# Nine edits to the order of work in a fused Fourier-mixing and SoLU kernel

## The chip, the cores and the metric

The kernel runs on one core of a Trainium2 chip. The metric is the device time of one execution in microseconds (us). The core has five engines that run side by side, each with its own instruction queue in program order: TensorE (PE, matrix products; its weight loads are listed as PEld), VectorE (DVE), ScalarE (ACT), GpSimd (POOL) and SyncE (SP, which here only issues DMAs). ACT and POOL issue DMAs too. [...]

## The reference

```python
X = np.fft.rfft(x, axis=1)                    # x: 8 x 3136 x 256
y = np.fft.irfft(X * (filt_r + 1j * filt_i), n=3136, axis=1)
x = y.reshape(25088, 256)
h = x @ w_in                                  # 256 -> 1024
e = np.exp(h - np.max(h, axis=-1, keepdims=True))
solu = h * (e / (np.sum(e, axis=-1, keepdims=True) + 1e-09))
mu = np.mean(solu, axis=-1, keepdims=True)
var = np.mean((solu - mu) ** 2, axis=-1, keepdims=True)
out = ((solu - mu) / np.sqrt(var + 1e-06) * g_ln) @ w_out   # 1024 -> 256
```

## The kernel before

**Two halves that overlap.** A prologue (up to about 150 us) transforms sequence 0 and prepares weights. Then one loop, `step(k)`, k from 0 to 204, carries 196 blocks of 128 tokens through the SoLU part, while the Fourier work of sequences 1 to 7 is dealt out into the same steps by the table `PLAN`. Two steps make a pair j (k = 2j is even, k = 2j + 1 is odd), since both products are done in Strassen's manner: seven products instead of eight for two blocks. Four blocks make a group g.

**The SoLU pipeline.** Steps 2j and 2j + 1 compute `product(j, 1..7)` into PSUM. The even step runs products 1, 2, 6, 7 and the odd one 5, 3, 4. Products 1, 6, 5, 3 pile up in one bank (`ms[j, 0]`); after each but the last, `keep` (ACT, L738) copies the running sum out, so the next product into that bank waits for the copy. `finish` (DVE, L749 and L752) adds the other banks. Two steps later `exponential` (ACT, L760) and `normalize` (DVE, L771 to L776) make the SoLU; three steps later `turn` (DVE, L792) transposes 32 x 32 blocks and `square` (ACT, L784) sums the variance. For a pair p = j - 3 the even step `regroup`s (eight DMAs on SP, L804) the turned blocks into `solu_t`; `project_sums` (POOL, L707) makes Strassen's sums from it. `project(p, m)` (PE, L849) multiplies by `w_out`: products 1, 2, 6, 7 of pair p = j - 4 in the odd step, and 5, 3, 4 of p = j - 5 in the even one. `keep_out` (ACT, L861) and `finish_out` (DVE, L865) scale the result by the row's 1/sigma, and `store_out` (two DMAs on SP, L873) writes it.

**The row factors.** 1/sigma of group g takes a detour through DRAM, since it has to be turned from rows to the regrouped order. `deviations` (two small POOL operations L811, L813 and one SP DMA, L815, `rows<-rs`) runs in even step 4g + 6. `regroup_deviations` (four SP DMAs of 0.5 KB, L821, `rs_t<-rows`) runs in odd step 4g + 7. The first reader is `keep_out(p, 0, (0, 0))` of p = 2g, right after `project(p, 1)` in odd step 4g + 9.

**The Fourier part.** At the end of a step stand `late`, `pcs`, `pas`, `pbs`, `pys`, in this order: pc is the inverse product of a spectrum unit (its two PSUM banks are copied out by ACT, L344), pa the first stage (copied by ACT, L269), pb the forward spectrum product, py the last stage (copied by ACT, L382, and joined by DVE, L390). pc and pb use the same two banks `ps_b`, one buffer each; pa and py share the two buffers of `ps_t`. `spectrum_loads` issues from ACT's queue the two loads of a spectrum unit (512 KB of `t2`, L286, and 256 KB of tables, L688), in the step before that unit's pb.

**What sets the order.** `tc.manual_schedule()`: every engine executes its instructions in the order in which `step` writes them. [...]

## Time and profile before

| | us |
|---|---|
| median of 3 runs | 1702.94 (1692.59 to 1709.13) |
| the profiled execution | 1712.57 |
| its span | 1710.8 |
| PE busy, share of the span | 1571.6, 92% |
| DVE busy | 1315.0, 77% |
| POOL busy | 1132.6, 66% |
| ACT busy | 906.7, 53% |

The difference of span and execution, 1.8 us, lies around the program. PE's busy time is partly modelled, so 92% says that PE rarely sits idle, not that it runs at its peak. In the chain of waits, which follows what ended last back to the start, the PE lines of the two token products, L849 and L728, hold 23% and 22% of the span, and DMAs 21%. The granted PE clock is full for all of the stretch from 550 to 1650 us. From about 1300 us on the Fourier work is over and only the SoLU part runs: there one sees a group of four steps undisturbed, 26.9 us long (the `turn` of 1516.3 and that of 1543.2 stand at the same place of the pattern).

### The profile page before, as it was taken

The page shows a single profiled execution, that of the slowest core. Times are in us where ns is not written, and L with a number is a line of the kernel's source. Part 1 is how long each engine was busy: PE and PEld are TensorE (multiplying, and loading weights), DVE is VectorE, ACT ScalarE, POOL GpSimd, SP SyncE. Part 2 cuts the span into 40 slices and gives each one's busy share as a digit, 9 for nine tenths or more (in the row PEclk, how much of TensorE's full clock was granted, in tenths as well). Part 3 has the DMA queues.
Part 4 walks back from the last instruction along what each step waited for, and adds up shares of the span by engine and source line. Part 5 has one row for each costly group of instructions (what it writes and reads, how often), then busy time and mean ns, then how long its engine had stood idle before and what let it go on. Part 6 is the DMA issues. An engine that isn't in the chain of part 4 may idle for free.

```text
span 1710.8 us, 36980 instructions
## 1 busy us (share of the span) xinstructions
PE 1571.6 (92%) x12710; PEld 1074.3 (63%) x12710; DVE 1315.0 (77%) x2642; ACT 906.7 (53%) x1772; POOL 1132.6 (66%) x1316
## 2 busy tenths in 40 slices
PE   5897889999889999999999999999999999999986
PEld 1353456666556676666666676666666677666666
DVE  1676877886678889887898788987888777777772
ACT  2134554565445655565556555565555565555552
POOL 4443686777566776787578766687666767666564
PEclk8999999999999999999999999999999999999998
DMA  9887877876788768865887678866775455343343
GB/s 259 250 269 228 239 208 201 220 209 167 170 223 200 195 188 233 225 182 150 201 239 193 171 175 220 220 180 166 199 223 133 123 127 121 101 100 97 94 106 93
DMA packets 377805, 312.13 MB, mean 182 GB/s; under 512 B 63322, under 2 KB 343395, under 8 KB 377619
## 3 DMA queue, kind: packets, MB, share of 16 engines
q1 hardware_dynamic: 306260, 169.81, 39.4%
q0 software_dynamic: 34464, 101.68, 20.8%
q10 hardware_dynamic: 36896, 38.28, 7.7%
q8 instruction: 103, 1.69, 0.4%
q14 instruction: 82, 0.67, 0.1%
HBM read 124.86 MB, written 81.50 MB: 121 GB/s over the span
## 4 chain that ended last, share of the span: by engine, by line
PE 54%; DMA 21%; DVE 11%; issue 6%; SPq 2%; ACT 2%; POOL 2%; ACTq 0%; DVEq 0%; POOLq 0%
PE o L849 23%; PE m L728 22%; DMA solu_t<-turn 6%; DMA x<-in_x_dram 3%; PE pb L296 2%; PE py L377 2%; DVE h L776 2%; DMA rs_t<-rows 2%; PE pc L296 2%; DMA t<-d 2%; DMA d<-x 2%; PE pa L264 2%; DMA rows<-rs 2%; DVE turn L792 1%; SPq L804 1%
## 5 line engine op out<-in xcount | busy, mean ns | idle before, releaser
L728 PE MATMUL m<-w_in_sb,s 128*128 128x512 f32 x784 | 397.1, 606 | 36.2 <-ACT h L738 28.9
L849 PEld LDWEIGHTS o<-w_out_sb,solu_t 128*128 128x128 f32 x3136 | 385.1, 194 | 54.4 <-issue 43.1
L849 PE MATMUL o<-w_out_sb,solu_t 128*128 128x128 f32 x3136 | 404.0, 278 | 8.3 <-DVE ot L865 8.3
L849 PEld LDWEIGHTS o<-w_out_sb,u 128*128 128x128 f32 x2352 | 307.6, 192 | 146.6 <-issue 129.9
L849 PE MATMUL o<-w_out_sb,u 128*128 128x128 f32 x2352 | 310.7, 275 | 10.0 <-ACT ot L861 10.0
L728 PE MATMUL m<-w_in_sb,y 128*128 128x512 f32 x588 | 310.3, 611 | 2.2 <-DVE nmax L752 2.2
L776 DVE SCALAR_TENSOR_TENSOR h<-e,rsum,h 128x1024 f32<-128x1024 f32 x196 | 306.6, 1564 | 6.9
L707 POOL TENSOR_TENSOR u<-solu_t 128x512 f32<-128x512 f32 x98 | 135.4, 1382 | 265.4 <-DMA solu_t<-turn 218.7
L861 ACT ACTIVATE ot<-o,rs_t 128x128 f32<-128x128 f32 x392 | 144.7, 369 | 265.2 <-PE o L849 240.5
L738 ACT COPY h<-m 128x512 f32<-128x512 f32 x294 | 171.1, 582 | 198.4 <-PE m L728 195.4
L784 ACT ACTIVATE h<-h,nmu 128x1024 f32<-128x1024 f32 x196 | 224.4, 1145 | 90.1 <-DVE turn L792 44.5
L792 DVE STREAM_TRANSPOSE turn<-h 128x1024 f32<-128x1024 f32 x196 | 242.5, 1237 | 2.1 <-DVE ot L865 0.3
L760 ACT ACTIVATE e<-h,nmax 128x1024 f32<-128x1024 f32 x196 | 224.9, 1148 | 22.4 <-DVE h L776 22.3
L728 PEld LDWEIGHTS m<-w_in_sb,s 128*128 128x128 f32 x784 | 130.5, 192 | 149.5 <-issue 96.8
L865 DVE SCALAR_TENSOR_TENSOR ot<-o,rs_t,ot 128x128 f32<-128x128 f32 x294 | 101.0, 344 | 148.8 <-ACT ot L861 121.9
L752 DVE CUSTOM_DVE_ANT_0 h<-m,h 128x512 f32<-128x512 f32 x196 | 134.2, 685 | 91.4 <-ACT h L738 88.0
L707 POOL TENSOR_TENSOR u<-solu_t,u 128x512 f32<-128x512 f32 x98 | 143.8, 1467 | 70.2 <-PE o L849 65.0
L707 POOL TENSOR_TENSOR solu_t<-solu_t,solu_t 128x512 f32<-128x512 f32 x98 | 142.5, 1454 | 7.7
L707 POOL TENSOR_TENSOR u<-u,solu_t 128x512 f32<-128x512 f32 x98 | 144.1, 1470 | 0.5
L728 PEld LDWEIGHTS m<-w_in_sb,y 128*128 128x128 f32 x588 | 96.7, 191 | 74.8 <-issue 49.1
L707 POOL TENSOR_TENSOR s<-y 128x128 f32<-128x128 f32 x196 | 100.4, 512 | 0.5
L318 DVE TENSOR_TENSOR pr<-pb,f 128x512 f32<-128x512 f32 (+1 forms) x53 | 34.3, 648 | 83.7 <-PE pb L296 60.3
(112 smaller groups left out, 2045.2 us busy)
## 6 DMA issues: line engine op xcount, KB each, us to landing
solu_t<-turn SPq DMA_DIRECT2D x784, 128.0 KB
out_dram<-ot SPq DMA_DIRECT2D x196, 128.0 KB
t<-d POOLq DMA_DIRECT2D x112, 200.0 KB, 6.0
d<-x POOLq DMA_DIRECT2D x100, 200.0 KB, 4.7
f<-f_dram POOLq DMA_DIRECT2D x39, 512.0 KB, 6.9
d<-g POOLq DMA_DIRECT2D x39, 512.0 KB, 4.9
t<-d ACTq DMA_DIRECT2D x36, 512.0 KB
x<-in_x_dram SPq DMA_DIRECT2D x112, 98.0 KB
```

What stands on the lines that cost most here:

```text
L296: nc.tensor.matmul(out=out[:, v, :], lhsT=lhsT(v), rhs=rhs[:, v, :], start=True, stop=True)
L707: nc.gpsimd.tensor_tensor(out=out, in0=in0, in1=in1, op=op)
L728: nc.tensor.matmul(out=ms[j, bank], lhsT=lhsT, rhs=w_in_sb[:, w, :], start=m in (1, 2, 7), stop=True, skip_group_check=True)
L738: nc.scalar.copy(out=h_half(k, i), in_=ms[j, 0])
L752: nc.vector.tensor_tensor_reduce(out=h_half(k, i), in0=ms[j, bank], in1=h_half(*kept), scale=1.0, scalar=sofar, op0=ALU.add, op1=ALU.min, ...
L760: nc.scalar.activation(out=e, in_=hs[k], func=AFT.Exp, bias=nmaxs.pop(k)[:, 1:2], scale=-1.0, accum_out=esum)
L776: nc.vector.scalar_tensor_tensor(out=solu, in0=e, scalar=rsum, in1=solu, op0=ALU.mult, op1=ALU.mult, accum_out=nmu)
L784: nc.scalar.activation(out=solu, in_=solu, func=AFT.Square, bias=nmu, scale=-float(DFF), accum_out=variances[g][:, i:i + 1])
L792: nc.vector.transpose(out=turns[g][:, :, i, :], in_=solus[k].rearrange("p (f j) -> p f j", j=32))
L849: nc.tensor.matmul(out=pos[p, bank], lhsT=lhs[:, f, :], rhs=w[:, f, :], start=f == 0 and m in (1, 2, 7), stop=True, skip_group_check=True)
L861: nc.scalar.activation(out=out_half(p, *to)[0], in_=pos[p, 0], func=AFT.Copy, scale=rs)
L865: nc.vector.scalar_tensor_tensor(out=ot, in0=pos[p, bank], scalar=rs, in1=out_half(p, *kept)[0], op0=ALU.mult, op1=ALU.add)
```

## The change

It moves work without changing what is computed:

1. `weight_sums(w_out_sb)`, four DVE subtractions at the end of step 5, becomes four POOL subtractions, one at the end of each of steps 4 to 7.
2. For sequence 1 in steps before 9, the closing add of a spectrum multiplication goes from DVE to POOL, and its second half from the end of step t to the start of step t + 1 (`tops`).
3. Even step: `exponential(k - 2)` goes behind `product(j, 1)` and `keep(j, k, 0)`.
4. Even step: `spectrum_loads` goes from behind `keep_out(p, 1, (0, 1))` to behind `project(p, 4)`, ahead of the regroups.
5. Even step: `regroup(j - 3, 0)` goes down to stand just ahead of `regroup(j - 3, 1)`.
6. `deviations(g)` goes from even step 4g + 6 to the start of odd step 4g + 7.
7. `regroup_deviations(g)` goes from odd step 4g + 7 to the very end of even step 4g + 8, behind `store_out`.
8. End of a step without pa: py goes ahead of pb.
9. In a step with pa but neither pb nor pc, py takes the two `ps_b` banks instead of `ps_t`.

```diff
+    def weight_sum(engine, w, n):
+        to, a, b = ((3, 6, 0), (5, 2, 6), (4, 2, 3), (6, 1, 4))[n]
+        engine.tensor_tensor(out=w[:, to], in0=w[:, a], in1=w[:, b], op=ALU.subtract)
...
-            weight_sums(w_out_sb)
+            weight_sum(nc.gpsimd, w_out_sb, step - 3)
...
-            parts = [lambda sp=sp, i=i, part=part: sp.multiply(i, part) for part in range(2)]
+            add = (nc.gpsimd if t + 1 < LAG else nc.vector).tensor_tensor
+            parts = [lambda sp=sp, i=i, part=part, add=add: sp.multiply(i, part, add) for part in range(2)]
...
-                (first_parts[t] if t + 1 < LAG else second_parts[t + 1]).append(parts[1])
+                (tops if t + 1 < LAG else second_parts)[t + 1].append(parts[1])
...
-            (pys[at] if e > 1 else late[t] if second_one else early[t]).append(lambda e=e, ch=ch: back_halves(
-                e, ch, [psum(f"py_{e}_{ch}_{g}") for g in range(2)]))
+            (pys[at] if e > 1 else late[t] if second_one else early[t]).append(
+                lambda e=e, ch=ch, at=at: back_halves(e, ch, psum_pair(f"py_{e}_{ch}", False)
+                                                      if pas[at] and not pbs[at] + pcs[at] else
+                                                      [psum(f"py_{e}_{ch}_{g}") for g in range(2)]))
...
-        for job in top[k] + stores[k] + differences[k] + products[k]:
+        for job in tops[k] + top[k] + stores[k] + differences[k] + products[k]:
             job()
         if odd and j + 1 < pairs:
             pair_sums(j + 1)
+        if odd and 0 <= j - 3 < pairs:
+            deviations(j - 3)
         if not odd:
-            if 2 <= k < blocks + 2:
-                exponential(k - 2)
             if hid:
                 product(j, 1)
                 keep(j, k, 0)
+            if 2 <= k < blocks + 2:
+                exponential(k - 2)
             if proj:
                 project(p, 5)
                 keep_out(p, 1, (0, 1))
-            for job in spectrum_loads[k]:
-                job()
...
-            if 0 <= j - 3 < pairs:
-                regroup(j - 3, 0)
...
                 project(p, 4)
+            for job in spectrum_loads[k]:
+                job()
             if 0 <= j - 3 < pairs:
+                regroup(j - 3, 0)
                 regroup(j - 3, 1)
-                deviations(j - 3)
...
                 store_out(p)
+            if 0 <= j - 4 < pairs and j % 2 == 0:
+                regroup_deviations((j - 4) // 2)
         else:
...
                 project_sums(j - 3, 0)
-                if (j - 3) % 2 == 0:
-                    regroup_deviations((j - 3) // 2)
...
-        for job in late[k] + pcs[k] + pas[k] + pbs[k] + pys[k] + loads[k]:
+        for job in late[k] + pcs[k] + (pas[k] + pbs[k] + pys[k] if pas[k] else pys[k] + pbs[k]) + loads[k]:
             job()
-        if k in (0, 1, 3, 5):
-            prepare_w_out((k + 1) // 2)
+        if k in (0, 1, 3, 4, 5, 6, 7):
+            prepare_w_out(k - (k > 2))
```

## The prediction

> **What bounds the kernel.** I read the page first: its engine line, the groups, then the chain of waits.

> ```profile
> span 1710.8 us, 36980 instructions
> PE 1571.6 (92%) x12710; PEld 1074.3 (63%) x12710; DVE 1315.0 (77%) x2642; ACT 906.7 (53%) x1772; POOL 1132.6 (66%) x1316
> ...
> L728 PE MATMUL m<-w_in_sb,s 128*128 128x512 f32 x784 | 397.1, 606 | 36.2 <-ACT h L738 28.9
> ```

> PE sets the time: 139 us of idle in 1711, some 46 of them before 155 us. The third line is the largest single idle of the loop: 28.9 us of waiting for `keep`. So every edit is priced by what it does to PE's queue. I then went through PE's list of waits, and next to the timelines of SP, PE and ACT over one undisturbed group, because edits 6 and 7 move DMAs on SP that ACT, and behind it PE, wait for. First SP (start, us, what, count):

> ```profile
> 1517.66 6.00 SPq L804 DMA_DIRECT2D solu_t<-turn  x8
> 1523.75 0.56 SPq L815 DMA_DIRECT2D rows<-rs  x1
> 1524.41 1.31 SPq L873 DMA_DIRECT2D out_dram<-ot  x2
> 1525.82 1.87 SPq L821 DMA_DIRECT2D rs_t<-rows  x4
> 1527.80 9.43 SPq L804 DMA_DIRECT2D solu_t<-turn  x8
> 1537.33 1.30 SPq L873 DMA_DIRECT2D out_dram<-ot  x2
> ```

> This is group 42: step 4g+6 ends with the first stores, 4g+7 is the four `rs_t` loads, 4g+8 is the second eight regroups and the second stores. The reader, on PE and ACT:

> ```profile
> 1533.57 1.06 PE L849 MATMUL o<-w_out_sb,solu_t 128*128 128x128 f32 x8
> 1534.46 1.88 PE L728 MATMUL m<-w_in_sb,s 128*128 128x512 f32 x4
> 1536.18 1.95 PE L849 MATMUL o<-w_out_sb,solu_t 128*128 128x128 f32 x16
> ...
> 1539.68 1.05 PE L849 MATMUL o<-w_out_sb,u 128*128 128x128 f32 x8
> ```
> ```profile
> 1536.38 0.58 ACT L738 COPY h<-m 128x512 f32<-128x512 f32 x1 [2.24 <-PE m L728]
> 1537.27 0.37 ACT L861 ACTIVATE ot<-o,rs_t 128x128 f32<-128x128 f32 x1 [0.31 <-PE o L849]
> 1537.54 1.14 ACT L760 ACTIVATE e<-h,nmax 128x1024 f32<-128x1024 f32 x1
> ```

> PE's lines are project 4 of step 4g+8; products 7 and 5; project 1 and 2 of step 4g+9; and, at 1539.68, project 6, which adds into the bank that `keep_out` must first have read. The reader of `rs_t` is the L861 at 1537.27. The loads ended issuing at 1527.7: even 3.3 us to land leaves 6 us to spare.

> [...] one `rs_t` load is a 0.47 us slice, while the chain of waits shows 3.3 us and more to landing (below). [...] the window below holds a 4.9 us wait of PE (the longest of pa L264 behind POOL) and its clock (0.93, before the last two columns) is down; from 550 to 1650 us, with no such wait, it is 1.00.

> ```profile
> 500.00:550.00 50.00, 43.45 (x412) 29.53 (x411) 37.85 (x72) 25.74 (x51) 30.95 (x38) 0.93 0.84 215
> ```

> **The change, part by part.**

> *Edit 7, the load of the row factors.* New place: behind the stores of step 4g+8, one step ahead of their first reader. SP can't get there sooner: the last four regroups overwrite a buffer that project 4 reads (SP sits until 1534.66, PE's project 4 ends at 1534.63), then come 4 x 0.65 = 2.6 us of regroups and 1.3 of stores. So the loads begin at 1538.7, after their reader's old time of 1537.27. The fourth begins 3 x 0.47 = 1.4 later, at 1540.1. Issue to landing, from the chain of waits (start, us):

> ```profile
> 1686.15 3.33 DMA rs_t<-rows
> ...
> 1219.47 8.28 DMA rs_t<-rows
> ```

> With 3.33 it lands at 1543.4; `keep_out` takes 0.37, the hand-over about 0.1: project 6 starts at 1543.9 and not at 1539.68, **4.2 us late**. Behind `keep_out` on ACT stand the exponential and all that follows; on DVE `finish_out` waits for it, with `turn` and two `finish` behind. Their 0.35 + 1.24 + 0.70 + 0.75 = 3.0 us put the next bank of product 1 free at about 1546.3, when PE's projects 6 and 7 (1.8 us) are over by 1545.7: 0.6 us more, which I drop[...]. The loop does not absorb the delay by running later: project 4, regroups, stores, loads, `keep_out` and project 6 are one chain inside one pair of steps.
> For the 15 groups after 1300 us: 15 x 4.2 = 63. For the 34 before, DMAs are crowded. Landing lies between 3.3 and 8.3; I take 1 us more. Edit 4 adds some 0.9 (below): 34 x 6.1 = 207. Sum **270**; bounds 49 x 2.8 = 137 (landing in 1.9, the shortest in the chain, and no crowding) and 63 + 34 x 8.5 = 352.
> [...]

> *Edit 6.* Two POOL operations (1.25 and 1.04 us in crowded steps) and one SP DMA of 0.56 move to the start of the odd step, behind `pair_sums`. POOL loses a wait of 91 us in all for ACT (row L811), SP loses 43.9 for `rows`: neither is on PE's path. On SP `rows` can now hold back the x loads and the next regroups by about 1 us; these have a step of slack. Nothing, as long as SP idles ahead of `turn` (181 us in all).

> *Edit 3.* In the even step the exponential (1.15) stood before `keep`, and product 6 waited: ACT ran 1529.89 to 1531.04, then the copy, though product 1 was done at 1528.93. Now the copy goes at once. Of the 28.9 us some 24 are at this place (the rest at product 5): **-24**. `normalize` needs the exponential only behind product 7.

> *Edits 8 and 9.* PE's waits name them: 10.5 us for `pb <- ACT g L344` (15 times, at most 0.7), 7.3 for `py <- ACT x L269` (16 times). 11 steps have pc, pb, py and no pa; py's 1.0 us fills the copy of pc there: 11 x 0.7 to 1.15, **-10**. 9 steps have pa and py alone; ps_b is free in them (pb is read until the next odd step's pc, and none is open): 9 x 0.9, **-8**. The 10 steps with all four stay as they are.

> *Edits 1 and 2.* DVE loses 2.62 (L145, at 167.67) and eight adds of 0.69 early on; PE waited 4.53 us at 172 behind that DVE queue. **-5**, bounds 0 and -12. POOL gains 4 x 1.4 and 8 x 1.4 us while it idles (23 of 50 us busy).

> *Edit 4.* ACT's two issues (0.37 each) move some 3.1 us down (from 1202.20 to behind the L861 that ends at 1205.30). The load's landing is not shown; POOL's loads of the same kind take 6.0 in the median, so 1202.2 + 3.1 + 0.8 + 6 = 1212, against pb at 1214.4: covered, with about 2 us to spare; with 10 us of landing each of 42 pb waits 2. But regroups queue behind this load's semaphore:

> ```profile
> SPq L804 <- DMA t<-d: 29.4, 12, 4.0
> ```

> A load 3.1 us later holds them longer, in 20 of the 34 early groups at the place that matters; half of that is 20 x 1.5 = 31, the 0.9 a group used above.

> *Edit 5.* SP's order is the same, as no SP instruction stood between: nothing.

> **The sum.** 270 + 55 - 24 - 10 - 8 - 5 = 278. Of the some 55 us of other PE waits in the loop a stop in every group swallows about half: -27. 1712.6 + 251 = 1964; the profiled execution lies 0.6% above the median of runs, so 1953, say **1955 us**.

> **The rivals.**
> *Hidden after all (faster).* If the loads landed before `keep_out` is due, only the gains stay: 1712.6 - 47 = 1666, less 0.6%: 1656. For it: that `rs_t` is hidden today in most groups (ACT waits for it 8.8 us in all). Against: SP must reach the loads 4.2 us sooner than project 4 allows; from there on it decides. Chance 0.06.
> *Late but soft.* The shortest landing (137), no loss of clock: 1712.6 + 137 - 47 - 27 = 1776, less 0.6%: 1765. For it: PE's clock survived waits of 1.7 us. Chance 0.08.
> *Late and dragging the spectrum loads with it.* 352 + 83 - 47 and 42 x 2 = 84 at pb: 1712.6 + 472 = 2185, less 0.6%: 2172, or half of these additions, about 2100. For it: SP's wait above, and 21% DMA in the chain. Against: PE's delay gives the loads time. Chance 0.07.
> *That an edit doesn't do what it says:* the ps_b choice may never be met. Then 8 us fall away, inside the range.

> **The numbers.** Forecast 0.79, around 1955. Range: from the sum with bare 4.2 in all groups and no clock (1712.6 + 206 - 74 = 1845, less 0.6%: 1834) to the upper bounds with nothing swallowed (1712.6 + 352 + 83 - 47 = 2101, less 0.6%: 2088): 1830 to 2085. A change of under 1%, 17 us, can't be told from none here, as three runs spread by that much. Faster 0.05, same 0.02, slower 0.93.

> **What would show it.** Right: L861 idle before `DMA rs_t<-rows`, several us in each group; PE's L849 `u` idle behind `ACT ot L861`, some 49 times; `rs_t<-rows` high in the chain; a PE clock below 1.00 after 550 us; `m <- ACT h L738` down to about 5 us; `pb <- ACT g` and `py <- ACT x` nearly gone. Wrong: an `rs_t` issue ahead of the stores, or L861 waiting for PE alone.

## The result, and the profile after

The changed kernel takes 2077.29 us (median of 4 runs, 2071.42 to 2079.66) against 1700.6 for the kernel before on the same chip: a ratio of 1.2209, 95% interval 1.2141 to 1.2277. It is slower by 377 us. The page of the changed kernel (span; busy time of the engines; the clock row; the two PE groups that answer to the question; line numbers are up by 5, so L849 is L854 and L861 is L866):

```profile
span 2073.4 us, 36674 instructions
...
PE 1658.6 (80%) x12710; PEld 1147.2 (55%) x12710; DVE 1280.4 (62%) x2630; ACT 903.1 (44%) x1772; POOL 1126.6 (54%) x1328
...
PEclk8998989999889898989998998998899898998997
...
L854 PE MATMUL o<-w_out_sb,u 128*128 128x128 f32 x2352 | 358.3, 302 | 349.8 <-ACT ot L866 349.7
...
L733 PE MATMUL m<-w_in_sb,s 128*128 128x512 f32 x784 | 389.2, 597 | 2.6 <-DVE rsum L776 1.6
```

No engine has more work to speak of (12 operations went from DVE to POOL), and every engine is less busy as a share. One group of PE, the projects whose left side is a sum (`u`), has 349.7 us of idle time behind `keep_out`; before it had 10.0. The wait for `keep` that the last line had (28.9 us) is gone. Three terms make up the span's 362.6 us:

| | before | after | difference |
|---|---|---|---|
| PE idle at the L849/L854 `u` group behind ACT | 10.0 | 349.7 | +339.7 |
| PE idle elsewhere | 129.2 | 65.1 | -64.1 |
| PE busy | 1571.6 | 1658.6 | +87.0 |

(PE idle is the span less PE busy: 139.2 and 414.8.) The last row is the same 12710 products, each longer on average, at a mean granted clock of 0.898 after 0.980 (worked out under "Clock" below).

A quiet group of the changed kernel, by the timelines of SP, PE and ACT (start, us, engine, line, what, count, idle time before it and what ended it):

```profile
1856.66 9.96 SPq L809 DMA_DIRECT2D solu_t<-turn  x8
1866.72 1.30 SPq L878 DMA_DIRECT2D out_dram<-ot  x2
1868.08 1.92 SPq L826 DMA_DIRECT2D rs_t<-rows  x4
```
```profile
1862.79 1.06 PE L854 MATMUL o<-w_out_sb,solu_t 128*128 128x128 f32 x8
...
1868.05 1.02 PE L733 MATMUL m<-w_in_sb,y 128*128 128x512 f32 x2
1873.18 2.05 PE L854 MATMUL o<-w_out_sb,u 128*128 128x128 f32 x8 [4.11 <-ACT ot L866]
```
```profile
1872.67 0.37 ACT L866 ACTIVATE ot<-o,rs_t 128x128 f32<-128x128 f32 x1 [6.48 <-DMA rs_t<-rows]
```

Read them in order of time: project 4 ends at 1863.85; SP ends its regroups and stores at 1868.02 and only then issues the loads; ACT's `keep_out` waits 6.48 us for them; project 6 waits 4.11 us for `keep_out`. In a crowded group the same chain is longer. SP stands from 1427.65 to 1432.37, until project 4 has ended, and with it all that follows on its queue. The four loads, 1.9 us in the quiet group, are spread over 6.73: SP stands 4.0 us ahead of the fourth, until 1442.99, when the regroup issued at 1433.01, eight DMAs earlier on SP, has landed. In this trace the 1513 DMAs of SP and the 114 of ACT complete on eight semaphores in all, and this load has the same one as that regroup:

```profile
1432.38 2.61 SPq L809 DMA_DIRECT2D solu_t<-turn  x4
1435.09 1.44 SPq L878 DMA_DIRECT2D out_dram<-ot  x2
1436.58 6.73 SPq L826 DMA_DIRECT2D rs_t<-rows  x4
```
```profile
1447.44 2.05 PE L854 MATMUL o<-w_out_sb,u 128*128 128x128 f32 x8 [9.87 <-ACT ot L866]
```

The same wait in the list of SP's waits over the whole run (what waits, for what; us in total, times, the longest):

```profile
SPq L826 <- DMA solu_t<-turn: 15.9, 16, 4.0
```

Taken over the 48 groups that have a project 4 ahead of them (means, us; the landing of the fourth load is read from its completion semaphore in the trace). "Quiet" are the last 15, behind the last spectrum load; "crowded" are the earlier ones; "spectrum" means that step 4g+8 also holds spectrum loads. The Fourier work is not quite over in the quiet ones: its last stage (py) runs until 1767 us here, and in the kernel before it ran until 1448, not only until 1300.

| from the end of project 4 | quiet, 15 groups | crowded, 11 | crowded, spectrum, 22 |
|---|---|---|---|
| regroups issued | 2.69 | 2.80 | 4.03 |
| stores issued | 1.47 | 1.45 | 1.94 |
| to the issue of the fourth load | 1.74 | 2.22 | 3.09 |
| its landing | 3.24 | 4.60 | 4.72 |
| `keep_out`, then project 6 starts | 0.68 | 0.65 | 0.65 |
| sum | 9.83 | 11.72 | 14.43 |

Unhindered, project 6 follows 5.05 us after the end of project 4 (1534.63 to 1539.68 before). The first three rows are SP's own time: 5.9, 6.5 and 9.1 us.

### The profile page after: what moved, and what is told of

Its sections match the earlier page's. It is cut to its first block, busy times and chain, and to the rows that moved or that the text cites. A ratio compares the mean times of both kernels' runs of the same rounds, so it can differ in the third digit from the quotient of the medians.

```text
span 2073.4 us, 36674 instructions
## 1 busy us (share of the span) xinstructions
PE 1658.6 (80%) x12710; PEld 1147.2 (55%) x12710; DVE 1280.4 (62%) x2630; ACT 903.1 (44%) x1772; POOL 1126.6 (54%) x1328
## 4 chain that ended last, share of the span: by engine, by line
PE 58%; DMA 24%; SPq 9%; DVE 4%; issue 2%; ACT 2%; POOL 0%; ACTq 0%; DVEq 0%; POOLq 0%
PE o L854 27%; PE m L733 19%; DMA rs_t<-rows 8%; DMA solu_t<-turn 7%; SPq L809 4%; PE pb L301 3%; SPq L826 3%; PE py L382 3%; PE pc L301 3%; DMA x<-in_x_dram 2%; DMA out_dram<-ot 2%; PE pa L269 2%; SPq L878 2%; DMA de<-de_tbl 1%; DMA t<-d 1%
## 5 line engine op out<-in xcount | busy, mean ns | idle before, releaser
L854 PE MATMUL o<-w_out_sb,u 128*128 128x128 f32 x2352 | 358.3, 302 | 349.8 <-ACT ot L866 349.7
L854 PEld LDWEIGHTS o<-w_out_sb,u 128*128 128x128 f32 x2352 | 343.6, 214 | 506.3 <-issue 357.4
L854 PEld LDWEIGHTS o<-w_out_sb,solu_t 128*128 128x128 f32 x3136 | 419.7, 208 | 45.5 <-issue 43.0
L854 PE MATMUL o<-w_out_sb,solu_t 128*128 128x128 f32 x3136 | 437.6, 292 | 0.7 <-DVE ot L870 0.7
L866 ACT ACTIVATE ot<-o,rs_t 128x128 f32<-128x128 f32 x392 | 143.4, 366 | 640.9 <-DMA rs_t<-rows 348.6
L733 PE MATMUL m<-w_in_sb,y 128*128 128x512 f32 x588 | 319.1, 627 | 6.2 <-DVE nmax L757 4.4
L781 DVE SCALAR_TENSOR_TENSOR h<-e,rsum,h 128x1024 f32<-128x1024 f32 x196 | 288.4, 1471 | 6.9
L712 POOL TENSOR_TENSOR u<-solu_t,u 128x512 f32<-128x512 f32 x98 | 165.2, 1686 | 229.3 <-PE o L854 225.7
L712 POOL TENSOR_TENSOR u<-solu_t 128x512 f32<-128x512 f32 x98 | 126.8, 1293 | 255.0 <-DMA solu_t<-turn 132.6
L712 POOL TENSOR_TENSOR solu_t<-solu_t,solu_t 128x512 f32<-128x512 f32 x98 | 131.4, 1341 | 7.7
L353 POOL DMA_DIRECT2D d<-g x46 | 36.8, 799 | 175.7 <-ACT g L349 153.9
```

Source lines behind the costliest of these rows:

```text
L712: nc.gpsimd.tensor_tensor(out=out, in0=in0, in1=in1, op=op)
L733: nc.tensor.matmul(out=ms[j, bank], lhsT=lhsT, rhs=w_in_sb[:, w, :], start=m in (1, 2, 7), stop=True, skip_group_check=True)
L781: nc.vector.scalar_tensor_tensor(out=solu, in0=e, scalar=rsum, in1=solu, op0=ALU.mult, op1=ALU.mult, accum_out=nmu)
L854: nc.tensor.matmul(out=pos[p, bank], lhsT=lhs[:, f, :], rhs=w[:, f, :], start=f == 0 and m in (1, 2, 7), stop=True, skip_group_check=True)
L866: nc.scalar.activation(out=out_half(p, *to)[0], in_=pos[p, 0], func=AFT.Copy, scale=rs)
```

## The experiments

Ratios are to the kernel before, with 95% intervals; its median lay between 1698.7 and 1702.0 us.

### Edits 6 and 7 undone, and edit 4 as well

```diff
 # step 4g+6, behind regroup(j - 3, 1)
+                deviations(j - 3)
 # step 4g+7, behind project_sums(j - 3, 0)
+                if (j - 3) % 2 == 0:
+                    regroup_deviations((j - 3) // 2)
 # start of the odd step, end of the even step
-            deviations(j - 3)
-                regroup_deviations((j - 4) // 2)
```

> The changed kernel with edits 6 and 7 undone: rows<-rs again in step 4g+6, rs_t<-rows again in step 4g+7; the other seven edits stay. Theory (the rs_t loads stand on SP behind regroups that project 4 holds back, and all of the loss is theirs): the whole loss goes and the gains of the other edits stay, 1630 to 1670 us, and ACT's waits for rs_t come to under 20 us. Rival (the later spectrum loads or another moved step cost a good part): above 1710 us.

Measured: 1662.53 us, 0.9775 (0.9717 to 0.9833). From the page:

```profile
PE 1557.4 (94%) x12710; PEld 1068.8 (64%) x12710; DVE 1292.6 (78%) x2630; ACT 902.7 (54%) x1772; POOL 1160.3 (70%) x1328
...
L854 PE MATMUL o<-w_out_sb,u 128*128 128x128 f32 x2352 | 312.8, 276 | 12.6 <-ACT ot L866 9.6
```

The whole loss sits in these two edits; the other seven make the kernel 36 us faster than before (1698.69 in this comparison). PE's wait at the `u` group is back at 9.6 us, and ACT waits for `rs_t` 15.1 us in all. With edit 4 undone too (spectrum loads back behind `keep_out(p, 1, (0, 1))`):

> The changed kernel with edits 4, 6 and 7 undone. Theory (the later spectrum loads cost something only where the rs_t loads stand behind the regroups that they hold; with these back in step 4g+7 SP's longer holds, 46 and 28 us behind the spectrum loads, are covered): within 8 us of the run with edits 6 and 7 undone, 1655 to 1670 us. Rival (edit 4 costs by itself): 1635 to 1652 us.

Measured: 1663.17 us, 0.9777 (0.9741 to 0.9813). Where the `rs_t` loads stand early, edit 4 costs and brings nothing that these runs can tell. These two are the fastest versions tried.

### Edit 7 alone

Edit 7 applied to the kernel before, nothing else.

> The kernel before with edit 7 alone. Theory: the whole loss is there without the other eight edits; 350 us of waits at project 6 and 87 us of halved clock, less some 25 to 70 us of waits that a stop in each group swallows: 2060 to 2120 us. Rival (edit 7 needs the later spectrum loads to become so dear): crowded groups lose 6 us and not 8 to 9, so 1960 to 2030 us.

Measured: 2098.83 us, 1.2337 (1.2276 to 1.2399). PE's waits:

```profile
PE o L849 <- ACT ot L861: 325.4, 53, 9.9
PE m L728 <- ACT h L738: 12.0, 15, 1.4
```

So edit 7 is enough for the loss. It also swallows 17 of the 28.9 us that PE waited for `keep`, without edit 3. The chain from project 4 to project 6 takes 9.96 us here in quiet groups and 11.75 in crowded ones, as in the changed kernel (9.83 and 11.72). Only in the 22 groups with spectrum loads does it differ, 13.43 against 14.43. That points to edit 4, whose later loads then add 1.0 us there; edit 4 was not undone alone. The rest of what crowded groups take beyond quiet ones is there without it.

### The loads in the same step, but first on SP

```diff
         if not odd:
+            if 0 <= j - 4 < pairs and j % 2 == 0:
+                regroup_deviations((j - 4) // 2)
             if hid:
                 product(j, 1)
...
                 store_out(p)
-            if 0 <= j - 4 < pairs and j % 2 == 0:
-                regroup_deviations((j - 4) // 2)
```

> The changed kernel with the four rs_t loads in the same step 4g+8, but at its start, ahead of the regroups on SP. Theory (the place behind the regroups and stores decides, not the step): the loads are issued some 8 us earlier and land before their reader, so 1630 to 1680 us. Rival (a step is too late in any case, landing takes too long beside the other transfers): PE still waits at project 6 for 2 us or more in most groups, above 1800 us.

Measured: 1718.66 us, 1.0096 (1.0068 to 1.0125). That is between the two: 359 us better than the changed kernel, 56 worse than with edits 6 and 7 undone. What is left shows in the waits of PE and of SP's queue:

```profile
PE o L854 <- ACT ot L866: 48.4, 22, 5.4
```
```profile
SPq L826 <- DMA rows<-rs: 196.4, 49, 7.4
```

SP stands at the loads in all 49 groups until `rows`, which edit 6 moved a step later, has landed, and the regroups wait behind. The same with edit 6 undone as well:

> The changed kernel with the four rs_t loads at the start of step 4g+8 and edit 6 undone, so that rows<-rs is issued in step 4g+6 again. Theory (the loss left in the run with the loads first comes from edit 6: SP stands at the loads until rows has landed, 196 us in all, and the regroups behind are late): that wait falls under 40 us and the time to 1645 to 1675 us, as with edits 6 and 7 undone. Rival (loads in step 4g+8 are too late for the crowded groups wherever they stand): still above 1695 us.

Measured: 1668.79 us, 0.9823 (0.9781 to 0.9865). That SP wait is now:

```profile
SPq L826 <- DMA rows<-rs: 30.1, 16, 6.1
```

One step before the reader is early enough, if the loads stand ahead of the regroups and `rows` was issued in step 4g+6.

### The same late place, another queue

`regroup_deviations` stays where the change put it, but `nc.sync.dma_start` in it becomes `nc.gpsimd.dma_start`.

> The changed kernel with the four rs_t loads at the same late place of the program, but issued from POOL's queue. Theory (what makes them late is the queue of SP, with regroups, stores and held semaphores ahead of them): POOL is past its sums soon after project 4 and needs no stores, so the chain from project 4 to project 6 shortens from 9.8 us in quiet groups and 11.7 to 14.4 in crowded ones by 2 to 4 us, and the time falls to 1840 to 1960 us. Rival (the late step alone decides, whatever the queue): 2040 us or more.

Measured: 1830.07 us, 1.0781 (1.0730 to 1.0831): 247 us of the loss go with the queue alone, and the time lies 10 us below the expected range. A quiet group on POOL, ACT and PE:

```profile
1619.99 2.13 POOL L712 TENSOR_TENSOR u<-solu_t,u 128x512 f32<-128x512 f32 x1 [2.13 <-PE o L854]
1622.07 2.25 POOL L826 DMA_DIRECT2D rs_t<-rows  x4
```
```profile
1626.45 0.37 ACT L866 ACTIVATE ot<-o,rs_t 128x128 f32<-128x128 f32 x1 [3.37 <-DMA rs_t<-rows]
```
```profile
1626.96 1.13 PE L854 MATMUL o<-w_out_sb,u 128*128 128x128 f32 x8 [1.00 <-ACT ot L866]
```

Nothing but one sum stands between project 4 (ended 1620.74) and POOL's loads. PE waits 1.00 us here, where it waited 4.11 in the quiet group above, and 129.6 in all after 349.7. By the means over quiet groups the fourth load is issued 3.1 us after project 4 instead of 5.9 and lands 3.0 us later instead of 3.2: the gain is in the issue, not in the landing. The chain is 6.8 us in quiet groups, 6.5 in crowded ones and 10.0 in those with spectrum loads.

### What the halved clock costs

The changed kernel, with project 2 of the waiting pairs done again, so that PE works during the wait. The first product of a project 2 is issued with `start` set, so that it begins the bank anew (`again` only keeps it from taking a new bank).

```diff
...
                 project(p, 2)
+                if p % 2 == 0:
+                    for _ in range(2):                # 4 in the second run
+                        project(p, 2, again=True)     # into the same bank
```

> The changed kernel, in which project 2 of the pairs that wait is done three times (the same result in the same bank, 32 more products of 0.111 us, 3.6 us of PE time inside a wait of 4 to 9 us). Theory of the clock (the halved clock after each stop costs PE some 87 us): [...] the mean clock rises from 0.90 towards 0.96, and the time falls by 30 to 80 us to 2000 to 2045. Rival (the halved clock falls into waits and costs nothing): the same 2077 us or more.

> The changed kernel with project 2 of the waiting pairs done five times (7.1 us of PE time more, against waits of 4 to 9 us). Theory of the clock: PE hardly stands still any more, the halved clock falls from 425 us to under 200 us, and where the crowded groups gain by that, the quiet ones lose some 3 us each, 15 in all, since 7.1 us is longer than their wait of 4.2: 2000 to 2060 us, pairs after the wait in crowded groups 0.5 to 1.5 us shorter. Rival (the clock costs nothing beside the wait): 2090 us or more, by the 3 us in quiet groups.

The sizes in both texts are twice too large: one project is 8 products of 0.111 us, so the runs add 1.8 and 3.6 us to a wait, not 3.6 and 7.1. Measured: 2067.04 us, 1.2148 (1.2073 to 1.2223), and 2035.34, 1.1963 (1.1914 to 1.2013). The first can't be told from the changed kernel: in the quiet groups but the last two PE still stood for 2.0 to 4.4 us, in most crowded ones longer, and by the clock records of the trace the clock was halved for 340 us, after 423 (mean clock 0.918 after 0.898). It misses what was expected and decides nothing. The second is clear: 42 us faster with 1568 more products. The clock is halved for 212 us (mean 0.948) and PE's waits behind `keep_out` fall to this:

```profile
PE o L854 <- ACT ot L866: 160.9, 52, 8.5
```

The wait itself is covered by useless work and hardly shortened: the chain from project 4 to project 6 takes 9.71, 11.48 and 14.34 us, which accounts for 6 of the 42 us. The rest goes with the clock after the wait: PE's busy time less the 174 us of added products is 44 us shorter (1788.1 less 174 against 1658.6). Two neighbouring groups of the changed kernel show the same by themselves (stretch; its length; busy time of PE, PEld, DVE, ACT, POOL; PE clock; DMA):

```profile
1828.80:1858.00 29.20, 25.33 (x142) 17.77 (x142) 18.30 (x43) 15.22 (x31) 16.82 (x19) 1.00 0.34 86
1858.00:1890.00 32.00, 27.73 (x142) 19.82 (x141) 19.30 (x43) 15.14 (x31) 18.31 (x19) 0.89 0.34 87
```

The first had a wait of 3.75 us and kept its clock, the second one of 4.11 us and lost it. PE is busy 2.4 us longer with the same 142 records; the other 0.4 us is the longer wait. But the length of the wait alone does not decide. Here are two waits of 3.75 us, the first the one just named, the second in the run with edit 7 alone, each with the eight products behind it, which take 1.13 us in the one and 1.62 in the other:

```profile
1843.23 1.13 PE L854 MATMUL o<-w_out_sb,u 128*128 128x128 f32 x8 [3.75 <-ACT ot L866]
```
```profile
1889.01 1.62 PE L849 MATMUL o<-w_out_sb,u 128*128 128x128 f32 x8 [3.75 <-ACT ot L861]
```

### The gains: edit 3 alone, edits 8 and 9 alone

Each applied to the kernel before, as in the diff of the change.

> The kernel before with edit 3 alone (keep ahead of the exponential in even steps). Theory: 24 of the 28.9 us of PE's waits for keep go and nothing takes their place: 1670 to 1682 us against 1700, PE m behind ACT h under 8 us. Rival (the wait moves to the projects' banks or to the exponential's readers): gain under 10 us.

Measured: 1684.78 us, 0.9904 (0.9871 to 0.9937): a gain of 15 us by the medians, between what the two theories named. One line of PE's waits tells why:

```profile
PE m L728 <- ACT h L738: 13.7, 10, 4.6
```

By the order of the products in the traces, 20 of the 29 waits stood at product 6, where edit 3 acts, with 17.2 us, and 8 at product 5, with 11.0. Here product 6 has none left, and product 5 has 9 with 12.9 us, the longest 4.6. So edit 3 did all that it could at its place, 17.2 less 1.9 us, and the prediction had read 24 us there.

> The kernel before with edits 8 and 9 alone (py between pc and pb, or in the banks of pb). Theory: PE's waits pb behind ACT g and py behind ACT x, 17.8 us together, come to under 5 us and the time falls by 12 to 20 us. Rival (what PE gains there it loses at the next wait for the bank or for the transfers): gain under 6 us.

Measured: 1677.21 us, 0.9887 (0.9847 to 0.9926): 22 us by the medians. Both waits are nearly gone:

```profile
PE pb L296 <- ACT g L344: 2.8, 4, 0.7
...
PE py L377 <- ACT x L269: 0.2, 1, 0.2
```

These waits fell by 15 us, from 17.8 to 3.0; the gain of 22 has an interval of 13 to 26. 15 and 22 make 37, and all seven edits bring 36 us (39 without edit 4), so edits 1, 2, 4 and 5 together bring about nothing that these runs can tell. Edits 1 and 2 were not tried alone.

## Why the prediction was right

The direction and the mechanism held: 2077 lies in the range of 1830 to 2085, near its upper end. The forecast of 1955 was too low by 122 us: PE's waits behind `keep_out` grew by 339.7 us where 270 was said, the clock cost 87 where 55 was said, and 64 us of other waits went where 74 was said. The last 10 us are a scaling: the forecast took off 0.6% because the profiled execution before was that much slower than the median, and the profiled execution after was not. Both large terms came out about at the upper bounds given for them (349.7 us of waits against 352, 87 against 83), so it is the bounds and not the middle that kept 2077 inside the range. Step by step:

- **Place of the loads.** Right within 0.4 us at each term in quiet groups: the prediction had project 4's end, 2.6 of regroups, 1.3 of stores, 1.4 to the fourth load, 3.33 to land, 0.5 to project 6. Measured are 2.69, 1.47, 1.74, 3.24 and 0.68. Project 6 is 4.8 us late where 4.2 was said; 15 x 4.8 = 72 against 63. (The chain before also held a landing in 1.90 us, so "3.3 us and more" was too firm; the prediction used the 1.9 as a bound.)
- **Crowded groups: the term that was mis-sized.** The prediction took 34 x 6.1 = 207. By the table they are 6.7 us late without spectrum loads and 9.4 with: 11 x 6.7 + 22 x 9.4 = 281, and with the quiet ones 353, the 349.7 of the page. The landing was sized well (4.6 and 4.7 where 4.3 was said), and edit 4 was not far off (22 us by the comparison with edit 7 alone, 31 said). What was left out are the holds on SP: in crowded groups regroups, stores and the loads themselves wait for an earlier DMA to land (15.9 us in 16 waits at the loads, by the list of SP's waits above), and in the groups with spectrum loads SP takes 9.1 us to the fourth load instead of 5.9. The prediction charged such holds to edit 4 alone, though with edit 7 alone they stand at 7.6.
- **Clock.** The 55 us in the prediction's sum and the 83 in its upper bound were an estimate of its author's, read from no trace. PE is 87 us longer busy over the same products. That fits the clock: PE was busy for 242 us of halved clock, after 49 before, and half of the difference, an estimate of its price, is 97. Of the 48 waits 46 brought half clock, mostly for more than one window: in the loop, halved stretches last 3.4 us (6 of 47) or a multiple of it (21 last 6.8, 16 last 10.2, 4 last 13.7). About 36 of the 42 us of the longer busy wait are the part that this experiment took back.
- **Gains.** 47 predicted, 36 to 39 measured. Edit 3 was put at 24 and brought 15: only 17.2 of the 28.9 us stood at its place, and that was misread. Edits 8 and 9 were put at 18 and brought 22. Edits 1 and 2 were put at 5 and brought nothing that shows.
- **Waits swallowed.** The gains and the 27 us swallowed make 74 in the prediction; PE's idle time elsewhere fell by 64. (The 46 us of idle time that the prediction puts before 155 us reach to 200; before 155 there are 36.)
- **Edit 5, edit 6: nothing.** For edit 6 that held, it seems, only because the loads came still later. Where the loads stood first, `rows` one step later cost about 50 us (1718.66 against 1668.79): the loads then held SP until `rows` had landed.
- **Rivals.** "Hidden after all" gave 1656 as the price without the wait; with the wait taken out, 1662.5 was measured. "Late but soft" gave 1765 with a landing in 1.9 us and no loss of clock; the landing took 3.24 us in the mean of the quiet groups and 4.6 to 4.7 in the crowded ones, and the mean clock fell from 0.980 to 0.898. "Late and dragging the spectrum loads with it" did not come about: PE waited for a spectrum load's data (`pb` behind DMA `t` and `de`) 14 us in all, after 12 before.

## What to carry to other kernels

A small transfer that feeds a wide engine belongs ahead of whatever its queue may stand still for (359 us here), but not ahead of its own source: the loads that stood first while `rows` was still on its way held the queue themselves, for 196 us in all. Follow the in-order queue back from its new place to the last thing it waits for: the reader can come no sooner than that, plus every issue in between, plus the landing (5.9 us and 3.24 here in quiet groups, behind project 4). When such a chain closes within one turn of a pipelined loop, as it does here, running later does not absorb it, and each turn pays again: 4.8 to 9.4 us in each of the 48 groups, and 87 us of longer products on top, at a mean clock of 0.898.

## What was not expected of the hardware

- Doing 3.6 us of useless products in a wait made the kernel 42 us faster (2077 to 2035); some 36 us of it go with the clock, halved for 212 us and not 423.
- Waits of a little under 4 us did not all end alike: one of 3.75 us, split over two windows of the 3.41 us grid, left the clock at 1.00; behind another of 3.75 us eight products took 1.62 us, not 1.13; and with one of 4.11 us came 6.8 us of half clock (1872.0 to 1878.9).
- The same 0.5 KB load, the fourth of its group, took 1.77 us from issue to landing in one quiet group of the kernel before (issued at 1556) and 4.52 in another (at 1339). In the quiet groups of the changed kernel, behind 0.75 MB of regroups and stores in SP's queue, it took 2.27 to 5.27, 3.24 in the mean.
